# Pinning TensorE's order in an attention stage, halving and spreading the w4 tiles, moving transposes ahead of projections, and warming the array

## The chip, the cores and the metric

The kernel runs on one core of a Trainium2 chip. The metric is the device time of one execution in microseconds (us). A time quoted below is the median of several executions. Each kernel also has a trace of one execution; its span is 1.6 to 1.8 us shorter than the time of that execution, because the span goes from the first to the last instruction only. Executions are sorted into a fast and a slow state (more than 1.5% above the fastest of the same kernel); ratios use fast ones, while the medians quoted hold all executions. Engines are named as in the profile: PE is TensorE, DVE is VectorE, ACT is ScalarE, SPq is the queue on which SyncE issues DMAs.

## The reference, cut to what matters

The input x has 2048 rows of 512. Two branches work on its layer norm: a local dilated attention (32 heads of 16, each query sees 8 keys at distance 0, 2, ..., 14), and a gated MLP.

```python
x  = A_x
xn = _layernorm(x)
s  = _A_ref(xn, A_wqkv, A_wo)         # q,k,v = xn @ wqkv; softmax over 8 keys; @ wo
g  = _silu(_B_ref(xn, B_w1, B_w2, B_w3, B_w4))
return x + s * g
# _B_ref: h = gelu(layernorm(x) @ w1); h shifted by rows; x1 = x + h @ w2
#         return x1 + gelu(layernorm(x1) @ w3) @ w4      (w3: 512 x 1376, w4: 1376 x 512)
```

## The kernel before

Because the dilation is 2, even and odd rows never meet in the attention, so the kernel splits x into two halves of 1024 rows (`p` = 0, 1). It has three stages.

1. For four chunks of 512 rows: layer norm on DVE, transposes on PE, the q/k projection, w1, w2, a second layer norm, w3.
2. The attention: 9 units for each half, 18 in all. A unit has 128 or 120 queries, the last of a half only 56. PE computes v (4 matmuls) and scores (16 small matmuls in four groups of 4). ACT takes the exponential of each group, DVE multiplies by the mask, and PE computes AV, the weighted values (32 small matmuls), whose result is copied out by ACT (first half of the heads) and DVE (second half). The 16 tiles of w4 (12 matmuls each) are woven in so that PE has work while ACT computes.
3. The tail: 16 output tiles with wo, the gate and the residual on DVE, and the stores.

The softmax's denominators come out of AV as extra rows. A "run" of units is normalised together: the denominators are stored to DRAM, loaded in another layout (`dn`), inverted on DVE (`rb`), stored, and loaded back as a broadcast (`rr`); a later DVE multiply on `oT` (`normalise_end`) applies them. `load_xo` loads 1 MB of x again for the residual of the tail. The library's scheduler may reorder instructions of one engine unless told otherwise.

```python
for cuts in ((0, 5, NU), (0, 5, 7, NU)):          # runs: five in all
    ...
sm4 = tc.tile_pool(name="sm4", bufs=5)            # prob and others
psA = tc.tile_pool(name="psA", bufs=3, space=PSUM)   # s_ps, o_ps
psB = tc.tile_pool(name="psB", bufs=2, space=PSUM)   # v_ps, w4_ps, wo_ps
...
def weighted(p, u, va, prs):
    ...
    op = psa("o_ps")
    for jj in range(2):
        for dt in range(ND):
            for cg in range(4):
                nc.tensor.matmul(op[32*cg : 32*cg+32, jj, dt*nq : (dt+1)*nq], ...)   # 16 per jj
        dst = orw[p][jj][:, :, q0 - ra : q0 - ra + nq]
        if jj == 0:
            nc.scalar.activation(dst, src, AF.Copy)
        else:
            nc.vector.tensor_copy(out=dst, in_=src)
    if u == runs[p][r][1] - 1:
        normalise(p, r)

def normalise(p, r):
    for jj in range(2):
        nc.sync.dma_start(out=hv[jj], in_=orw[p][jj][DH : P : 32, :, 0:rw])
    nc.sync.dma_start(out=dn, in_=den_d...)
    ...
    nc.vector.reciprocal(out=rb, in_=dn)
    nc.sync.dma_start(out=rden_d..., in_=rb)
    for dt in range(ND):
        nc.sync.dma_start(out=rr[:, dt, 0:rw], in_=rden_d[8*dt : 8*dt+8, :]...broadcast)

def normalise_end(p, r):
    nc.vector.tensor_tensor(out=oT..., in0=oT..., in1=rrs[p, r]..., op=ALU.mult)
...
fill = {n: [w4s[n]] for n in range(13)}           # one whole w4 tile in each of units 0 to 12
fill[5].append(lambda: load_xo(0))
fill[9].append(lambda: load_xo(1))
fill[9].append(lambda: normalise_end(0, 0))
fill[13] = [lambda: normalise_end(0, 1)]
fill[17] = [lambda: normalise_end(1, 0)]
prev = None
for n, (p, u) in enumerate(order):
    cur = (p, u) + scores(p, u)                   # v, then the scores
    for f in fill.get(n, ()):
        f()
    if prev is not None:
        weighted(*prev)                           # AV of the unit before
    prev = cur
weighted(*prev)
for f in w4s[13:]:
    f()                                           # the last three w4 tiles
```

The softmax here doesn't subtract the row's maximum and nothing guards it: scores larger than these inputs give would overflow.

## Time and profile before

The kernel took 259.66 us, the median of three executions (258.02 to 260.58). The stages are read from PE's timeline: the first matmul of the attention and the first of wo bound the second stage.

| what | before |
|---|---|
| traced span | 258.0 us |
| stage 1, until the first attention matmul | 119.5 us |
| stage 2, attention and w4 | 115.6 us |
| stage 3, from the first wo matmul to the end | 22.9 us |

From the page of the kernel before: PE's busy time with its share of the span and number of instructions; the busy share of PE and the clock granted to it in 40 slices of 6.45 us, in tenths (9 is 90% or more); and the start of the line about the chain of work that ended last.

```profile
PE 222.5 (86%) x1704; PEld 98.3 (38%) x1704; DVE 152.8 (59%) x275; ACT 136.0 (53%) x164; POOL 39.9 (15%) x82
...
PE   0399898958999999999999999785999988799882
...
PEclk9999999997999999999999999998699999569999
...
PE 56%; DVE 15%; ACT 10%; DMA 9%; issue 4%; POOL 3%; SPq 2%; DVEq 0%; ACTq 0%
```

PE is the engine to look at: 86% busy, and most of the chain. But it is not at its best: the start is empty, some slices in the attention show 8, 7 or less, and the clock falls to 8, 6 and 5 in places (a matmul then takes longer and still counts as busy: ten w4 matmuls behind a fall are busy 4.45 us instead of 2.33, as shown below). So the busy share says little here about how far the kernel is from its best: the change below took 6% off the time and moved the busy share only from 86% to 88%.

From PE's timeline of the kernel before, in stage 1. Columns: start and length in us, engine, line, operation, output<-inputs, size, number of instructions grouped; in brackets the idle time before and what ended it.

```profile
13.66 8.84 PE L234 MATMUL qk_ps<-xnT_133,wqk_sb 128*128 128x512 bf16 x30
...
58.37 0.27 PE L222 MATMUL rrep_ps<-diag,ones_bf 128*128 128x128 bf16 x2 [3.12 <-DVE xnT_134 L215]
59.03 3.17 PE L234 MATMUL qk_ps<-xnT_134,wqk_sb 128*128 128x512 bf16 x7 [0.40 <-DVE xnT_134 L215]
```

PE's first work, 16 transposes, comes at 8.86 us, and the first projections run slowly (30 matmuls in 8.84 us, 0.29 each; later ones take 0.22). Their starts are 0.43 us apart until about 18 us and 0.21 us after. The clock row does not show this (it has 9 in these slices), so a cold start has to be read from durations. At 58 us PE has nothing to do for 3.12 us because the transposed data of the last chunk have not been copied out of PSUM by DVE.

The same view, over one unit of the attention with a whole w4 tile.

```profile
141.77 0.39 PE L397 MATMUL o_ps<-prob,v_aug_129 128*32 128x120 bf16 x16
142.09 0.82 PE L349 MATMUL v_ps<-wv_sb,xnT_133 128*128 128x512 bf16 x3
142.98 0.39 PE L397 MATMUL o_ps<-prob,v_aug_129 128*32 128x120 bf16 x16
...
144.52 0.39 PE L327 MATMUL w_ps<-w_sb,h3T 128*128 128x512 bf16 x1
145.07 0.38 PE L369 MATMUL s_ps<-qm_137,kT_135 32*128 32x240 bf16 x4 [0.17 <-ACT prob L376]
145.38 2.33 PE L327 MATMUL w_ps<-w_sb,h3T 128*128 128x512 bf16 x10
```

The AV matmuls (`o_ps`) come in two groups of 16 with v between them. The w4 tile sits mostly behind all the scores (x10). Between the score groups there is one w4 matmul. One such unit takes 6.1 us.

DVE's timeline of the kernel before, around PE's largest hole in the attention.

```profile
174.34 1.43 DVE L447 TENSOR_TENSOR oT_1500<-oT_1500,rr 128x2432 bf16<-128x2432 bf16 x1 [2.83 <-DMA rr<-rden_d_1502]
175.68 0.65 DVE L408 CAST orw<-o_ps 128x480 bf16<-128x480 f32 x1
176.25 0.67 DVE L353 CAST v_aug_129<-v_ps 64x512 bf16<-64x512 f32 x1
```

PE's timeline at the same place:

```profile
176.98 0.81 PE L349 MATMUL v_ps<-wv_sb,xnT_134 128*128 128x512 bf16 x3 [2.54 <-DVE v_aug_129 L353]
...
180.83 4.45 PE L327 MATMUL w_ps<-w_sb,h3T 128*128 128x512 bf16 x10
```

DVE works in order here: it waited 2.83 us for the broadcast load `rr` with the copies of AV and v behind it (at 175.68 and 176.25), so PE had a hole of 2.54 us. After the hole ten w4 matmuls took 4.45 us, against 2.33 us in an undisturbed unit: the granted clock over 180 to 190 us is 0.73.

### The profile page before, as it was taken

To read this page: it belongs to the slowest core of one execution; us is meant where nothing else is said; L and a number is where in the kernel's file an instruction comes from. 1 tells how busy PE (TensorE), PEld (TensorE's weight loads), DVE (VectorE), ACT (ScalarE), POOL (GpSimd) and SP (SyncE) were. 2 spreads that over 40 slices of the span, in tenths; PEclk is the share of its full clock that TensorE was granted. 3 is DMA by queue.
4 is the path that set the end of the run, shared out by engine and by line. 5 is a ranking of instruction groups with operands and counts; after the bars stand their busy time and mean duration, and the time that the engine had idled before them with its cause. 6 is when DMAs were issued, how large, how long until landed. Compare 5 with 4: busy or idle time off the path is not lost.

```text
span 258.0 us, 4290 instructions
## 1 busy us (share of the span) xinstructions
PE 222.5 (86%) x1704; PEld 98.3 (38%) x1704; DVE 152.8 (59%) x275; ACT 136.0 (53%) x164; POOL 39.9 (15%) x82
## 2 busy tenths in 40 slices
PE   0399898958999999999999999785999988799882
PEld 0334444433444444444334433232333333334330
DVE  6688815087069571001766776538566977936994
ACT  1037575702813436567977777464477899603000
POOL 1526320001001110000000006000050006514100
PEclk9999999997999999999999999998699999569999
DMA  6998000002301734102200006160042005232343
GB/s 193 363 400 295 3 0 0 3 0 81 81 0 40 206 81 125 40 1 69 94 3 0 3 1 105 45 229 0 3 76 73 0 3 104 59 96 59 100 150 122
DMA packets 27628, 21.31 MB, mean 83 GB/s; under 512 B 12184, under 2 KB 26712, under 8 KB 27608
## 3 DMA queue, kind: packets, MB, share of 16 engines
q1 hardware_dynamic: 24152, 16.85, 21.0%
q0 software_dynamic: 1280, 2.10, 4.7%
q10 hardware_dynamic: 2176, 2.10, 2.3%
q8 instruction: 13, 0.21, 0.4%
q14 instruction: 7, 0.06, 0.1%
HBM read 12.39 MB, written 4.46 MB: 65 GB/s over the span
## 4 chain that ended last, share of the span: by engine, by line
PE 56%; DVE 15%; ACT 10%; DMA 9%; issue 4%; POOL 3%; SPq 2%; DVEq 0%; ACTq 0%
PE w_ps L311 14%; PE w_ps L327 13%; PE qk_ps L234 9%; ACT prob L376 7%; PE w_ps L278 5%; PE w_ps L250 4%; PE s_ps L369 4%; DVE l1s L179 3%; DMA rr<-rden_d_1502 2%; PE o_ps L397 2%; PE v_ps L349 2%; DVE orw L408 2%; SPq L439 1%; DMA oT_2286<-orw 1%; ACT orw L406 1%
## 5 line engine op out<-in xcount | busy, mean ns | idle before, releaser
L376 ACT ACTIVATE prob<-s_ps 128x960 bf16<-128x960 f32 (+2 forms) x72 | 61.8, 951 | 18.2 <-PE s_ps L369 15.2
L327 PE MATMUL w_ps<-w_sb,h3T 128*128 128x512 bf16 (+1 forms) x176 | 49.1, 412 | 0.2
L379 DVE TENSOR_TENSOR prob<-prob,mask_126 128x1920 bf16<-128x1920 bf16 (+1 forms) x32 | 34.8, 1088 | 16.7 <-ACT prob L376 16.6
L311 PE MATMUL w_ps<-x1nT,w_sb 128*128 128x512 bf16 (+1 forms) x176 | 38.3, 379 | 0.0
L316 ACT ACTIVATE h3T<-w_ps 128x1024 bf16<-128x1024 f32 x20 | 20.5, 1023 | 25.6 <-PE w_ps L311 23.3
L311 PEld LDWEIGHTS <-w_sb 128*128 128x128 bf16 (+1 forms) x176 | 17.6, 100 | 20.4
L327 PEld LDWEIGHTS <-h3T 128*128 128x128 bf16 (+1 forms) x176 | 16.1, 102 | 22.6 <-issue 9.4
L429 POOL DMA_DIRECT2D oT_1500<-orw x16 | 8.3, 526 | 86.3 <-ACT orw L406 86.3
L234 PEld LDWEIGHTS <-wqk_sb 128*128 128x128 bf16 x128 | 13.4, 107 | 18.3 <-issue 5.0
L353 DVE CAST v_aug_129<-v_ps 128x512 bf16<-128x512 f32 (+1 forms) x9 | 6.1, 681 | 23.0 <-PE v_ps L349 23.0
L333 ACT ACTIVATE sig<-w_ps 128x512 bf16<-128x512 f32 x16 | 9.6, 600 | 17.5 <-PE w_ps L331 17.4
L234 PE MATMUL qk_ps<-xnT_133,wqk_sb 128*128 128x512 bf16 x64 | 17.0, 428 | 1.1 <-DVE xnT_133 L215 1.1
L429 POOL DMA_DIRECT2D oT_2286<-orw x24 | 12.1, 512 | 36.9 <-ACT orw L406 35.2
L240 ACT ACTIVATE qm_137<-qk_ps,hmask 128x1024 bf16<-128x1024 f32 x8 | 8.4, 1112 | 17.7 <-PE qk_ps L234 17.7
L234 PE MATMUL qk_ps<-xnT_134,wqk_sb 128*128 128x512 bf16 x64 | 16.1, 409 | 0.7 <-DVE xnT_134 L215 0.7
L283 DVE TENSOR_TENSOR xn_85<-w_ps,xn_85 128x1024 bf16<-128x1024 f32 x4 | 4.9, 1216 | 18.4 <-PE w_ps L278 18.4
L369 PE MATMUL s_ps<-qm_138,kT_136 32*128 32x240 bf16 (+2 forms) x144 | 12.6, 278 | 3.5 <-ACT prob L376 1.7
L240 ACT ACTIVATE qm_138<-qk_ps,hmask 128x1024 bf16<-128x1024 f32 x8 | 8.3, 1114 | 13.6 <-PE qk_ps L234 13.6
L250 PE MATMUL w_ps<-xn2T,w_sb 128*128 128x512 bf16 x64 | 14.5, 379 | 0.0
L408 DVE CAST orw<-o_ps 128x480 bf16<-128x480 f32 (+2 forms) x18 | 11.2, 625 | 3.6 <-PE o_ps L397 3.0
L349 PE MATMUL v_ps<-wv_sb,xnT_134 128*128 128x512 bf16 (+1 forms) x36 | 11.1, 385 | 2.5 <-DVE v_aug_129 L353 2.5
L369 PE MATMUL s_ps<-qm_137,kT_135 32*128 32x240 bf16 (+2 forms) x144 | 10.2, 260 | 3.0 <-DVE orw L408 1.6
(107 smaller groups left out, 284.3 us busy)
## 6 DMA issues: line engine op xcount, KB each, us to landing
w_sb<-in_B_w_dram SPq DMA_DIRECT2D x1, 1376.0 KB
w_sb<-in_B_w_dram SPq DMA_DIRECT2D x1, 1280.0 KB
xn_85<-in_A_x_dram SPq DMA_DIRECT2D x4, 256.0 KB, 7.1
wqk_sb<-in_A_wqkv_dram SPq DMA_DIRECT2D x2, 512.0 KB
w_sb<-in_B_w_dram SPq DMA_DIRECT2D x2, 512.0 KB
xn_86<-in_A_x_dram SPq DMA_DIRECT2D x4, 256.0 KB
xo_1463<-in_A_x_dram SPq DMA_DIRECT2D x1, 1024.0 KB
xo_1830<-in_A_x_dram SPq DMA_DIRECT2D x1, 1024.0 KB
```

Of the source, the lines that this page charges most:

```text
L234: nc.tensor.matmul(pt[:, b, :], lhsT=wqk_sb[:, dt, nt * P : (nt + 1) * P], rhs=xnT[p][:, dt, cs], start=(dt == 0), stop=(dt == ND - 1),)
L240: nc.scalar.activation(qm[p][:, 2 * a : 2 * a + 2, e, cs], pt, AF.Copy, scale=hmask[:, e : e + 1])
L250: nc.tensor.matmul(pt[:, b, :], lhsT=w1_sb[:, dt, g * P : (g + 1) * P], rhs=xn2T[:, dt, :], start=(dt == 0), stop=(dt == ND - 1),)
L311: nc.tensor.matmul(pt[:fs, ft % 2, :], lhsT=w3_sb[:, dt, ft * P : ft * P + fs], rhs=x1nT[:, dt, :], start=(dt == 0), stop=(dt == ND - 1),)
L316: last["gelu"] = nc.scalar.activation(h3T[:, 2 * a : 2 * a + 2, :], pt, AF.Gelu_apprx_tanh)
L327: nc.tensor.matmul(pt, lhsT=h3T[:fs, ft, jj * P : (jj + 1) * P], rhs=w4_sb[:fs, ft, :], start=(ft == 0), stop=False,)
L349: nc.tensor.matmul(vp[:nk, :], lhsT=xnT[p][:, dt, k0 : k0 + nk], rhs=wv_sb[:, dt, :], start=(dt == 0), stop=(dt == ND - 1),)
L369: nc.tensor.matmul(st[:nk, b, dl * 2 * nq : (dl + 1) * 2 * nq].rearrange("k (e q) -> k e q", e=2), lhsT=kT[p][r : r + 32, dt, k0 : k0 + nk ...
L376: nc.scalar.activation(prv[:nk, jj], st[:nk, :, 0 : 4 * nq], AF.Exp, scale=SCALE)
L379: nc.vector.tensor_tensor(out=ph[:nk], in0=ph[:nk], in1=msk[:nk, 0:nq].unsqueeze(1).to_broadcast([nk, 16, nq]), op=ALU.mult,)
L408: nc.vector.tensor_copy(out=dst, in_=src)
L429: nc.gpsimd.dma_start(out=oT[p][DH * hh : DH * (hh + 1), :, ra : ra + rw], in_=orw[p][jj][32 * cg : 32 * cg + DH, :, 0:rw],)
```

## The change

It has four intents: warm the array before the data arrive; put the transposes of the next chunk ahead of the projections of the current one, so that DVE's copies are hidden; split each w4 tile in two and spread the halves over all units; and fix PE's order in the attention (`pin` queues an instruction behind the one traced before it on its engine) with AV as one group of 32. It also normalises in six runs rather than five, and asks for the multiplies earlier after their runs. The diff, cut to its core:

```diff
-    for cuts in ((0, 5, NU), (0, 5, 7, NU)):
+    for cuts in ((0, 4, 7, NU), (0, 4, 7, NU)):
-    sm4 = ... bufs=5
+    sm4 = ... bufs=6
@@ loads of the first chunk: four of 128 KB instead of two of 256 KB
+        n = 1 if c == 0 else 2
+        for t0 in range(k * TPC, (k + 1) * TPC, n):
@@ warm-up
+    wm = psA.tile([P, 2, CH], F32, name="warm_ps", tag="a")
+    for i in range(16):
+        nc.tensor.matmul(wm[:, i % 2, :], lhsT=ones_bf[:], rhs=ones_bf...broadcast to 512, ...)
@@ stage_a is split: stage_a1 = transposes, rrep, xn2T; stage_a2 = q/k projection, w1
     stage_ln(0)
-    stage_a(0)
+    stage_a1(0)
     stage_ln(1)
+    stage_a1(1)
+    stage_a2(0)
     stage_ln(2)
-    stage_a(1)
+    stage_a1(2)
+    stage_a2(1)
     ...
@@ attention
+    def pin(ins):
+        return tc.keep_in_program_order(ins)
     # all v, score, AV, w4 and wo matmuls: nc.tensor.matmul(...) -> pin(nc.tensor.matmul(...))
     # w4_tile returns [half(0, NF // 2), half(NF // 2, NF)]: 5 matmuls, then 6 + 1
     # scores(p, u) -> values(p, u) and scores(p, u, dd) for two groups each
@@ weighted: both AV halves, then both copies
+        for jj in range(2):
             dst = orw[p][jj][:, :, q0 - ra : q0 - ra + nq]
...
+    halves = [h for w in w4s for h in w]
+    NH = 28
+    fill = {n: ([], []) for n in range(2 * NU)}
+    for i in range(NH):
+        m = i * 36 // NH
+        fill[m // 2][m % 2].append(halves[i])
+    fill[6][1].append(lambda: load_xo(0))
+    fill[10][1].append(lambda: load_xo(1))
+    fill[7][1].append(lambda: normalise_end(0, 0))
+    fill[10][1].append(lambda: normalise_end(0, 1))
+    fill[12][1].append(lambda: normalise_end(0, 2))
+    fill[16][1].append(lambda: normalise_end(1, 0))
+    va = values(*order[0])
     for n, (p, u) in enumerate(order):
-        cur = (p, u) + scores(p, u)
-        for f in fill.get(n, ()):
-            f()
+        prs = [scores(p, u, 0)]
+        for f in fill[n][0]:
+            f()
+        prs.append(scores(p, u, 1))
+        for f in fill[n][1]:
+            f()
         if prev is not None:
             weighted(*prev)
-        prev = cur
+        prev = (p, u, va, prs)
+        if n + 1 < len(order):
+            va = values(*order[n + 1])
```

More of the change, by code (lines that the diff above doesn't have):

```diff
@@ L73 @@
     sm5 = ctx.enter_context(tc.tile_pool(name="sm5", bufs=4))
-    sm4 = ctx.enter_context(tc.tile_pool(name="sm4", bufs=5))
+    sm4 = ctx.enter_context(tc.tile_pool(name="sm4", bufs=6))
     fin = ctx.enter_context(tc.tile_pool(name="fin", bufs=2))
@@ L95 @@
         p, k = c // 2, c % 2
-        for h in range(2):
-            t0 = k * TPC + 2 * h
+        n = 1 if c == 0 else 2
+        for t0 in range(k * TPC, (k + 1) * TPC, n):
             nc.sync.dma_start(
-                out=xn[p][:, t0 : t0 + 2, :],
-                in_=xv[p, t0 * P : (t0 + 2) * P, :].rearrange("(i q) d -> q i d", q=P),
+                out=xn[p][:, t0 : t0 + n, :],
+                in_=xv[p, t0 * P : (t0 + n) * P, :].rearrange("(i q) d -> q i d", q=P),
             )
@@ L130 @@
     nc.vector.memset(nhalf[:], -0.5)
+    wm = psA.tile([P, 2, CH], F32, name="warm_ps", tag="a")
+    for i in range(16):
+        nc.tensor.matmul(
+            wm[:, i % 2, :], lhsT=ones_bf[:], rhs=ones_bf.unsqueeze(1).to_broadcast([P, TPC, P]),
+            start=True, stop=True,
+        )
     hmask = const.tile([P, 2], F32, name="hmask")
@@ L200, in stage_ln, with stage_a1 @@
         r2s[c] = r2
-    def stage_a(c):
+    xn2Ts = {}
+    def stage_a1(c):
         p, k = c // 2, c % 2
@@ L228, in stage_a, with stage_a2 @@
         )
+        xn2Ts[c] = xn2T
+    def stage_a2(c):
+        p, k = c // 2, c % 2
+        cs = slice(k * CH, (k + 1) * CH)
+        xn2T = xn2Ts.pop(c)
         for a in range(ND):
@@ L318, in stage_w3, with half @@
                 last["gelu"] = nc.scalar.activation(h3T[:FL, NF - 1, :], pt[:FL, 0, :], AF.Gelu_apprx_tanh)
+    def pin(ins):
+        return tc.keep_in_program_order(ins)
     def w4_tile(c, jj):
         p, i = c // 2, (c % 2) * TPC + jj
-        h3T = h3[c]
-        pt = psB.tile([P, D], F32, name="w4_ps", tag="b")
-        for ft in range(NF):
-            fs = P if ft < NF - 1 else FL
-            nc.tensor.matmul(
-                pt, lhsT=h3T[:fs, ft, jj * P : (jj + 1) * P], rhs=w4_sb[:fs, ft, :],
-                start=(ft == 0), stop=False,
-            )
-        nc.tensor.matmul(pt, lhsT=ident[:], rhs=xn[p][:, i, :], start=False, stop=True)
-        sig = fin.tile([P, D], BF16, name="sig", tag="sig")
-        nc.scalar.activation(sig, pt, AF.Tanh, scale=0.5)
-        nc.vector.scalar_tensor_tensor(
-            out=xn[p][:, i, :], in0=sig, scalar=1.0, in1=pt, op0=ALU.add, op1=ALU.mult
-        )
+        st = {}
+        def half(lo, hi):
+            if lo == 0:
+                st["pt"] = psB.tile([P, D], F32, name="w4_ps", tag="b")
+            pt = st["pt"]
+            for ft in range(lo, hi):
+                fs = P if ft < NF - 1 else FL
+                pin(
+                    nc.tensor.matmul(
+                        pt, lhsT=h3[c][:fs, ft, jj * P : (jj + 1) * P], rhs=w4_sb[:fs, ft, :],
+                        start=(ft == 0), stop=False,
+                    )
+                )
+            if hi == NF:
+                pin(nc.tensor.matmul(pt, lhsT=ident[:], rhs=xn[p][:, i, :], start=False, stop=True))
+                sig = fin.tile([P, D], BF16, name="sig", tag="sig")
+                nc.scalar.activation(sig, pt, AF.Tanh, scale=0.5)
+                nc.vector.scalar_tensor_tensor(
+                    out=xn[p][:, i, :], in0=sig, scalar=1.0, in1=pt, op0=ALU.add, op1=ALU.mult
+                )
+        return [lambda: half(0, NF // 2), lambda: half(NF // 2, NF)]
     cnt = {"v": 0}
@@ L341, with values @@
     orw = {}
-    def scores(p, u):
+    def values(p, u):
         q0, nq, k0, nk = units[u]
@@ L348, in scores @@
         for dt in range(ND):
-            nc.tensor.matmul(
-                vp[:nk, :], lhsT=xnT[p][:, dt, k0 : k0 + nk], rhs=wv_sb[:, dt, :],
-                start=(dt == 0), stop=(dt == ND - 1),
+            pin(
+                nc.tensor.matmul(
+                    vp[:nk, :], lhsT=xnT[p][:, dt, k0 : k0 + nk], rhs=wv_sb[:, dt, :],
+                    start=(dt == 0), stop=(dt == ND - 1),
+                )
             )
@@ L355, in scores @@
         )
+        return va
+    def scores(p, u, dd):
+        q0, nq, k0, nk = units[u]
         msk = mask0 if u == 0 else mask1
-        prs = []
-        for t in range(4):
-            dd, jj = t // 2, t % 2
-            if jj == 0:
-                pr = sm4.tile([P, H * P // 2], BF16, name="prob", tag="s4")
-                prv = pr[:, 0 : H * nq // 2].rearrange("p (t b x) -> p t b x", t=2, b=2)
-                prs.append(pr)
+        pr = sm4.tile([P, H * P // 2], BF16, name="prob", tag="s4")
+        prv = pr[:, 0 : H * nq // 2].rearrange("p (t b x) -> p t b x", t=2, b=2)
+        for jj in range(2):
             st = psa("s_ps")
@@ L368, in scores @@
                     dt = 2 * dd + dl
-                    nc.tensor.matmul(
-                        st[:nk, b, dl * 2 * nq : (dl + 1) * 2 * nq].rearrange("k (e q) -> k e q", e=2),
-                        lhsT=kT[p][r : r + 32, dt, k0 : k0 + nk],
-                        rhs=qm[p][r : r + 32, dt, :, q0 : q0 + nq],
-                        start=True, stop=True, tile_position=(r, 0),
+                    pin(
+                        nc.tensor.matmul(
+                            st[:nk, b, dl * 2 * nq : (dl + 1) * 2 * nq].rearrange("k (e q) -> k e q", e=2),
+                            lhsT=kT[p][r : r + 32, dt, k0 : k0 + nk],
+                            rhs=qm[p][r : r + 32, dt, :, q0 : q0 + nq],
+                            start=True, stop=True, tile_position=(r, 0),
+                        )
                     )
@@ L376, in scores @@
                 nc.scalar.activation(prv[:nk, jj], st[:nk, :, 0 : 4 * nq], AF.Exp, scale=SCALE)
-            if jj == 1:
-                ph = pr[:, 0 : 16 * nq].rearrange("p (h q) -> p h q", q=nq)
-                nc.vector.tensor_tensor(
-                    out=ph[:nk], in0=ph[:nk],
-                    in1=msk[:nk, 0:nq].unsqueeze(1).to_broadcast([nk, 16, nq]), op=ALU.mult,
-                )
-        return va, prs
+        ph = pr[:, 0 : 16 * nq].rearrange("p (h q) -> p h q", q=nq)
+        nc.vector.tensor_tensor(
+            out=ph[:nk], in0=ph[:nk],
+            in1=msk[:nk, 0:nq].unsqueeze(1).to_broadcast([nk, 16, nq]), op=ALU.mult,
+        )
+        return pr
     def weighted(p, u, va, prs):
@@ L396, in weighted @@
                     pi = jj * 8 + b * 4 + (dt % 2) * 2 + e
-                    nc.tensor.matmul(
-                        op[32 * cg : 32 * cg + 32, jj, dt * nq : (dt + 1) * nq],
-                        lhsT=va[:nk, dt * 8 + 4 * jj + cg, :],
-                        rhs=prs[dt // 2][:nk, pi * nq : (pi + 1) * nq],
-                        start=True, stop=True, tile_position=(0, 32 * cg),
+                    pin(
+                        nc.tensor.matmul(
+                            op[32 * cg : 32 * cg + 32, jj, dt * nq : (dt + 1) * nq],
+                            lhsT=va[:nk, dt * 8 + 4 * jj + cg, :],
+                            rhs=prs[dt // 2][:nk, pi * nq : (pi + 1) * nq],
+                            start=True, stop=True, tile_position=(0, 32 * cg),
+                        )
                     )
+        for jj in range(2):
             dst = orw[p][jj][:, :, q0 - ra : q0 - ra + nq]
@@ L459, in final_tile @@
         for dt in range(ND):
-            nc.tensor.matmul(
-                pt, lhsT=oT[p][:, dt, i * P : (i + 1) * P], rhs=wo_sb[:, dt, :],
-                start=(dt == 0), stop=(dt == ND - 1),
+            pin(
+                nc.tensor.matmul(
+                    pt, lhsT=oT[p][:, dt, i * P : (i + 1) * P], rhs=wo_sb[:, dt, :],
+                    start=(dt == 0), stop=(dt == ND - 1),
+                )
             )
@@ L474 @@
     stage_ln(0)
-    stage_a(0)
+    stage_a1(0)
     stage_ln(1)
+    stage_a1(1)
+    stage_a2(0)
     stage_ln(2)
-    stage_a(1)
+    stage_a1(2)
+    stage_a2(1)
     stage_ln(3)
-    stage_a(2)
+    stage_a1(3)
+    stage_a2(2)
     stage_b(0)
-    stage_a(3)
+    stage_a2(3)
     stage_b(1)
@@ L489 @@
     stage_w3(3)
-    w4s = [lambda c=c, jj=jj: w4_tile(c, jj) for c in range(NCH) for jj in range(TPC)]
-    fill = {n: [w4s[n]] for n in range(13)}
-    fill[5].append(lambda: load_xo(0))
-    fill[9].append(lambda: load_xo(1))
-    fill[9].append(lambda: normalise_end(0, 0))
-    fill[13] = [lambda: normalise_end(0, 1)]
-    fill[17] = [lambda: normalise_end(1, 0)]
+    w4s = [w4_tile(c, jj) for c in range(NCH) for jj in range(TPC)]
+    halves = [h for w in w4s for h in w]
[10 more added lines that the diff above has]
+    fill[16][1].append(lambda: normalise_end(1, 0))
     order = [(p, u) for p in range(2) for u in range(NU)]
+    va = values(*order[0])
     prev = None
     for n, (p, u) in enumerate(order):
-        cur = (p, u) + scores(p, u)
-        for f in fill.get(n, ()):
+        prs = [scores(p, u, 0)]
[3 more added lines that the diff above has]
+        for f in fill[n][1]:
             f()
@@ L506 @@
             weighted(*prev)
-        prev = cur
+        prev = (p, u, va, prs)
+        if n + 1 < len(order):
+            va = values(*order[n + 1])
+    for h in halves[NH : NH + 2]:
+        h()
     weighted(*prev)
-    for f in w4s[13:]:
-        f()
+    for h in halves[NH + 2 :]:
+        h()
     for i in range(M // P):
```

## The prediction

> **What bounds the kernel now.** TensorE: 222.5 of 258.0 us busy on the page, the chain of waits 56% PE. Three stages, from the PE timeline:
> 1. 0 to 119.5 us, projections, MLP up to w3. The first transposes wait until 8.9 us. The array then starts cold: 16 transposes take 1.89 us (1.06 later), 30 qk matmuls 8.84 us (6.64 later). Before each next chunk's projections PE waits for transpose copies on DVE (0.34+0.33 us twice; 3.12+0.40 us at 54 to 59 us).
> 2. 119.5 to 235.1 us, attention with w4. A unit with a whole w4 tile takes 6.1 us: about 5.4 us PE, the rest waits for exp (0.16), the DVE copy of the AV result (0.2 to 0.5), and the second AV half behind ScalarE's copy of the first (0.24). Units 13 to 16 have no w4 and go at 3.9 us, bound by ScalarE (4 exp at 0.86 plus a copy). After low PE use or the 2.5 us hole at 174.5 us the granted clock falls (0.73 in 180-190, 0.51 in 220-230): ten w4 matmuls take 4.45 us instead of 2.33. The hole is DVE waiting in order for the normalisation's broadcast load (to 174.3).
> 3. The tail, 22.9 us: 16 output tiles, bound by DVE (0.60+0.35 us each), and the last store.
>
> **What the change does.**
> Stage 1: 16 dummy matmuls before the data arrive (ones ready at 1.06 us) take no time that is needed and warm the array: -3 us. [...] Transposes ahead of projections hide the copies: -5 us. Smaller first loads: -0.5 us. DVE must normalise chunks 1 and 2 earlier and is nearly full there, so I give back 1 us. Together about -8 us.
> Stage 2: 28 w4 halves over 36 slots instead of 13 tiles in units 0 to 12 and three at the end. By durations above, a unit costs PE about 4.4 us on average (v 0.97, scores 2x0.32, AV 0.65, w4 9.3x0.216, switches), ScalarE 4.3, DVE 4.4. No engine has slack, so I expect about 4.9 us per full unit, 81 us for all, plus 3 us start and 6 us of w4 and AV after: 90 us. Against it: normalisation now is six runs; its DVE operations stand in order about one unit after the DMAs start, while the chain store-load-reciprocal-store-broadcast took 12.5 us here. I expect DVE to stand 2 to 4 us several times, worst at the second run of half 0, whose multiply follows the third run's copies. PE sees about half, and one or two stalls may still drop the clock for about 10 us (4 us lost each). So 101 us instead of 115.6: -14 us.
> Stage 3: unchanged, within 1 us.
>
> Only PE gaps, cold matmuls and throttling go away; the work is equal.
>
> **Predicted: 238 us, 80% between 230 and 248. Faster by over 2%: 0.95; within 2%: 0.04; slower: 0.01.**
>
> **Checks.** First qk matmuls at 0.22 us each, first attention matmul near 111 us; PE busy through 10 to 111 us without gaps. Full attention units 4.6 to 5.5 us; granted clock above 0.9 in most attention slices; longest DVE waits at the reciprocal and the normalisation multiply. Tail 21 to 24 us.
>
> **What would make it wrong.** Normalisation waits of DVE exposed in full (up to 15 us), with throttling after each: 248 us or more. Waits hidden and clock kept: 230 us. If pinning makes PE stand behind a late AV group, units stay at 6 us.

The terms of stage 1 come to -3 - 5 - 0.5 + 1 = -7.5, rounded to -8. The -3 us of the warm-up agree with the durations listed under 1 (1.89 - 1.06 and 8.84 - 6.64, together 3.03 us). The 10 us at a low clock behind a stall, with 4 us lost, are the author's estimate; the trace of the kernel before shows means of 0.73 and 0.51 over 10 us each, which makes 2.7 and 4.9 us of full clock lost.

## More of the kernel before

SyncE's DMA queue of the kernel before (the length is the issuing time only):

```profile
165.60 0.39 SPq L455 DMA_DIRECT2D xo_1830<-in_A_x_dram  x1
166.04 2.54 SPq L439 DMA_DIRECT2D rr<-rden_d_1502  x4
```

## The result, and the profile after

The changed kernel took 244.34 us (median of four, 242.17 to 245.36); the kernel before took 259.51 us in the same rounds. The ratio is 0.9408, with a 95% interval of 0.9329 to 0.9487: faster. A ratio here is the mean time of one kernel's fast runs over that of the other's fast runs of the same rounds, so it is not quite the ratio of the medians that are quoted. The outputs agree with the reference.

| stage | before | after | difference | predicted difference |
|---|---|---|---|---|
| 1 | 119.5 | 109.8 | -9.7 | -8 |
| 2 | 115.6 | 110.6 | -5.0 | -14 |
| 3 | 22.9 | 22.2 | -0.7 | 0 |
| span | 258.0 | 242.6 | -15.4 | -22 |

So the total fell into the predicted range, but the second stage gave a third of what was expected of it. From the page after, the lines that answer to those above (slices of 6.07 us).

```profile
PE 213.3 (88%) x1720; PEld 93.2 (38%) x1720; DVE 152.0 (63%) x277; ACT 136.1 (56%) x164; POOL 43.0 (18%) x90
...
PE   8789999999999999999788983998797897699892
...
PEclk9999999999999999999999998699979999889999
...
PE 48%; DMA 18%; DVE 13%; ACT 7%; issue 5%; SPq 5%; POOL 2%; DVEq 0%; ACTq 0%
```

PE's slices 4 to 19 are now full, but the second half still has 7s and 8s, a 3 in slice 25 (146 to 152 us), and the clock still drops to 6 once. In the chain PE's share fell from 56% to 48%, and that of DMA rose from 9% to 18%: the chain now goes through transfers. That is the first hint of where the expected gain went.

PE's timeline after, in stage 1.

```profile
1.12 6.14 PE L134 MATMUL warm_ps<-ones_bf 128*128 128x512 bf16 x16 [1.12 <-DVE ones_bf L128]
8.16 1.36 PE L222 MATMUL tr_ps<-ident,xn_85 128*128 128x128 bf16 x16 [0.90 <-DVE xn_85 L203]
...
11.89 5.12 PE L249 MATMUL qk_ps<-xnT_152,wqk_sb 128*128 128x512 bf16 x23
18.12 0.40 PE L222 MATMUL tr_ps<-ident,xn_85 128*128 128x128 bf16 x4 [1.10 <-DVE xn_85 L203]
```

The dummies fill 1.12 to 7.26 us, and the first projections run at 5.12/23 = 0.22 us each. The last chunk's projections (32 matmuls from 51.09 to 58.00 us) follow without a gap; the hole of 3.12 us is gone. PE's busy time by windows shows the sum. From its first transpose to the attention PE was busy 104.3 of 110.6 us before, and 99.3 of 101.6 us after. So of the 9.7 us, 0.7 are the earlier first transpose (8.86 to 8.16), 4.1 less waiting, and 4.9 shorter work at a better clock.

A unit of the attention after, in the same view.

```profile
130.17 0.60 PE L428 MATMUL o_ps<-prob,v_aug_148 128*32 128x120 bf16 x32
130.82 1.02 PE L377 MATMUL v_ps<-wv_sb,xnT_152 128*128 128x512 bf16 x4
131.77 0.39 PE L399 MATMUL s_ps<-qm_156,kT_154 32*128 32x240 bf16 x8
133.00 0.59 PE L399 MATMUL s_ps<-qm_156,kT_154 32*128 32x240 bf16 x8 [0.84 <-DVE orw L441]
```

AV is one group of 32, v follows whole, and the w4 half (x6, from 133.52 us, 1.47 us long) sits where the change put it. Nothing moves into the 0.84 us in which the second pair of score groups waits for a PSUM buffer that DVE's copy of AV has to free. Keep that wait in mind for one of the experiments.

DVE's timeline after, around its longest DMA wait of the attention.

```profile
147.81 0.92 DVE L468 RECIPROCAL rb<-dn 128x122 bf16<-128x122 bf16 x1 [4.41 <-DMA dn<-den_d_1417]
148.64 2.16 DVE L409 TENSOR_TENSOR prob<-prob,mask_145 128x1920 bf16<-128x1920 bf16 x2
150.72 1.22 DVE L441 CAST orw<-o_ps 128x480 bf16<-128x480 f32 x2
...
156.10 1.18 DVE L480 TENSOR_TENSOR oT_1416<-oT_1416,rr 128x1952 bf16<-128x1952 bf16 x1 [1.90 <-DMA rr<-rden_d_1418]
```

PE's timeline at the same place:

```profile
146.98 0.38 PE L399 MATMUL s_ps<-qm_156,kT_154 32*128 32x240 bf16 x4
151.42 0.58 PE L399 MATMUL s_ps<-qm_156,kT_154 32*128 32x240 bf16 x4 [4.07 <-DVE orw L441]
151.94 2.74 PE L350 MATMUL w_ps<-w_sb,h3T 128*128 128x512 bf16 x6
```

DVE stood 4.41 us at the reciprocal. Its next operations, two masks and two AV copies, ran back to back as soon as it went on; at 156.10 it waited 1.90 us more, for `rr`. PE's next score group waited 4.07 us for one of those copies. Then the six w4 matmuls took 2.74 us, against 1.47 in the unit shown before, at a clock of 0.68 (150 to 160 us). Why was `dn` late? The timeline of SyncE's DMA queue after (here the length is the issuing time only):

```profile
138.70 0.44 SPq L488 DMA_DIRECT2D xo_1566<-in_A_x_dram  x1
141.49 0.34 SPq L458 DMA_DIRECT2D dn<-den_d_1417  x1
```

The chain of work over this stretch, in order of time (start and length in us, what; a DMA's length runs to its landing):

```profile
138.13 3.30 DMA den_d_1417<-orw
...
141.49 6.30 DMA dn<-den_d_1417
```

The 1 MB residual load was issued at 138.70, and the small `dn` load at 141.49 took 6.30 us until DVE could start. In the kernel before, `dn` loads took 1.8 to 2.4 us to landing. The other multiplies of the attention waited too, each for its `rr`: 1.90, 2.17, 2.47 and 2.19 us. In sum DVE waited about 14 us for DMAs in the attention, against 7.5 us before.

### The profile page after: what moved, and what is told of

It reads as the page before. It is cut to its first block, busy times and chain, and to the rows that moved or that the text cites. A ratio compares the mean times of both kernels' runs of the same rounds, so it can differ in the third digit from the quotient of the medians.

```text
span 242.6 us, 4350 instructions
## 1 busy us (share of the span) xinstructions
PE 213.3 (88%) x1720; PEld 93.2 (38%) x1720; DVE 152.0 (63%) x277; ACT 136.1 (56%) x164; POOL 43.0 (18%) x90
## 4 chain that ended last, share of the span: by engine, by line
PE 48%; DMA 18%; DVE 13%; ACT 7%; issue 5%; SPq 5%; POOL 2%; DVEq 0%; ACTq 0%
PE w_ps L326 15%; PE qk_ps L249 9%; ACT prob L407 6%; PE w_ps L293 6%; PE w_ps L265 6%; PE w_ps L350 5%; SPq L472 3%; DVE prob L409 3%; DMA xn_85<-in_A_x_dram 3%; DMA dn<-den_d_1417 3%; PE v_ps L377 2%; DMA dn<-den_d_1877 2%; PE wo_ps L494 2%; PE s_ps L399 1%; DMA rr<-rden_d_1418 1%
## 5 line engine op out<-in xcount | busy, mean ns | idle before, releaser
L407 ACT ACTIVATE prob<-s_ps 128x960 bf16<-128x960 f32 (+2 forms) x72 | 62.5, 930 | 20.0 <-PE s_ps L399 19.9
L350 PE MATMUL w_ps<-w_sb,h3T 128*128 128x512 bf16 (+1 forms) x176 | 46.5, 403 | 3.2 <-DVE xn_85 L359 2.4
L409 DVE TENSOR_TENSOR prob<-prob,mask_145 128x1920 bf16<-128x1920 bf16 (+1 forms) x32 | 34.5, 1085 | 10.8 <-ACT prob L407 10.6
L462 POOL DMA_DIRECT2D oT_1416<-orw x24 | 12.3, 522 | 73.4 <-ACT orw L439 73.2
L350 PEld LDWEIGHTS <-h3T 128*128 128x128 bf16 (+1 forms) x176 | 15.8, 101 | 24.3 <-issue 11.4
L462 POOL DMA_DIRECT2D oT_2229<-orw x24 | 12.1, 512 | 38.9 <-ACT orw L439 38.0
L249 PEld LDWEIGHTS <-wqk_sb 128*128 128x128 bf16 x128 | 12.1, 98 | 12.8
L249 PE MATMUL qk_ps<-xnT_152,wqk_sb 128*128 128x512 bf16 x64 | 15.4, 379 | 0.8 <-DVE xnT_152 L224 0.8
L249 PE MATMUL qk_ps<-xnT_153,wqk_sb 128*128 128x512 bf16 x64 | 14.5, 379 | 0.0
L399 PE MATMUL s_ps<-qm_156,kT_154 32*128 32x240 bf16 (+2 forms) x144 | 8.8, 271 | 6.2 <-DVE orw L441 5.7
L377 PE MATMUL v_ps<-wv_sb,xnT_153 128*128 128x512 bf16 (+1 forms) x36 | 9.9, 399 | 3.6 <-DVE xn_86 L359 3.6
L399 PE MATMUL s_ps<-qm_157,kT_155 32*128 32x240 bf16 (+2 forms) x144 | 9.2, 265 | 3.6 <-ACT prob L407 2.4
```

What stands on the lines that cost most here:

```text
L249: nc.tensor.matmul(pt[:, b, :], lhsT=wqk_sb[:, dt, nt * P : (nt + 1) * P], rhs=xnT[p][:, dt, cs], start=(dt == 0), stop=(dt == ND - 1),)
L350: nc.tensor.matmul(pt, lhsT=h3[c][:fs, ft, jj * P : (jj + 1) * P], rhs=w4_sb[:fs, ft, :], start=(ft == 0), stop=False,)
L377: nc.tensor.matmul(vp[:nk, :], lhsT=xnT[p][:, dt, k0 : k0 + nk], rhs=wv_sb[:, dt, :], start=(dt == 0), stop=(dt == ND - 1),)
L399: nc.tensor.matmul(st[:nk, b, dl * 2 * nq : (dl + 1) * 2 * nq].rearrange("k (e q) -> k e q", e=2), lhsT=kT[p][r : r + 32, dt, k0 : k0 + nk ...
L407: nc.scalar.activation(prv[:nk, jj], st[:nk, :, 0 : 4 * nq], AF.Exp, scale=SCALE)
L409: nc.vector.tensor_tensor(out=ph[:nk], in0=ph[:nk], in1=msk[:nk, 0:nq].unsqueeze(1).to_broadcast([nk, 16, nq]), op=ALU.mult,)
```

## The experiments

The leading theory was that the missing 9 us are normalisation waits: DVE works in order (at 147.81 us above, masks and copies ran behind the 4.41 us wait), the change asks for reciprocals and multiplies before their data have landed, and the 1 MB load makes one of them much later. The rival was that the pinned order itself costs: PE stands behind a late AV or score group and nothing may move forward. Smaller questions were what the warm-up, stage 1 and the spreading of the halves are worth. Three calls ran on three different chips; the kernel before ran with each (medians 259.24, 259.20 and 258.76 us), so medians of different calls are comparable to about half a microsecond. Stage times come from one traced execution of each kernel, which varies too: the two traces of the changed kernel have 110.6 and 109.1 us in stage 2, and in the 12 traces that have the new stage 1 with the warm-up the attention starts at 109.6 to 110.9 us.

### e1_no_warm: the change without the dummies

```diff
-    wm = psA.tile([P, 2, CH], F32, name="warm_ps", tag="a")
-    for i in range(16):
-        nc.tensor.matmul(wm[:, i % 2, :], ...)
```

> The changed kernel without the 16 dummy matmuls. Theory (the dummies only warm the array while the data arrive): the 16 first transposes take about 1.9 us again and the first thirty qk matmuls about 8.8 us, attention starts 2 to 3.5 us later than the 109.8 us of the changed kernel, 247 us in all. Rival (the dummies buy nothing; stage 1 gains by its order alone, or DVE bounds the start): attention starts within 1 us of 109.8 us, 244 us.

Measured: 245.0 us, ratio 0.9454 (0.941 to 0.9499); the attention starts at 111.67 us instead of 109.8. PE's timeline of this run:

```profile
13.14 7.07 PE L242 MATMUL qk_ps<-xnT,wqk_sb 128*128 128x512 bf16 x23
```

The same 23 projections take 7.07 us instead of 5.12, and the 16 transposes 1.89 instead of 1.36. But the warm kernel then waits 1.10 us at 18.12 (shown above) and 0.41 us at 20.54, because DVE has not finished the next chunk; the cold one does not wait there. The warm-up brings 1.9 us at the start of the attention against the changed kernel's trace, and 0.8 to 2.1 against all twelve; that is just short of the 2 to 3.5 us of the theory and more than its rival allowed. In the total time the intervals of the two kernels overlap, so it is not resolved there. The 1.9 us are 0.8% of the span of 243 us.

### e2_stage1_only: the new stage 1 with the old attention

```diff
 (on the kernel before)
+ four first loads, the 16 dummies, stage_a1/stage_a2 in the new order
```

> The new stage 1 (dummies, smaller first loads, transposes ahead of projections) with the attention stage of the kernel before (its order, its runs, five buffers in the shared pool). Theory (the two parts add up; stage 1 is worth 9.7 us and attention 5): attention starts near 110 us and takes 115 us as before, 249 to 250 us in all. Rival (the parts need each other, the old attention starting earlier runs into later loads or another throttle phase): below 246 or above 253 us.

Measured: 248.23 us, ratio 0.9576 (0.9531 to 0.9622); two of its six executions were slow, and the four fast ones lie between 247.84 and 248.33 us. The trace is of a slow execution (251.73 us), so only its start is used: the attention begins at 109.82 us. So stage 1 is worth 11 us of the time, 1 us more than the stage table says and than was expected, and the new attention only about 4 to 5 us. Within that the parts add up; the missing gain is in the attention.

### e3_xo_late: the residual loads behind the last normalisation of half 0

```diff
-        nc.sync.dma_start(out=xo[p], ...)
+        pin(nc.sync.dma_start(out=xo[p], ...))
-    fill[6][1].append(lambda: load_xo(0))
-    fill[10][1].append(lambda: load_xo(1))
+    fill[12][1].append(lambda: load_xo(0))     # behind normalise_end(0, 2)
+    fill[12][1].append(lambda: load_xo(1))
```

> The changed kernel with both residual loads (1 MB each) pinned behind the broadcast of the third run of half 0, that is after about 182 us instead of at 138.7 and 170.1 us. Theory (the 4.4 us wait of DVE for the first denominator load is that load queueing behind the 1 MB transfer, and the half clock after it follows from the hole): that wait falls below 1 us, the 4.1 us hole of TensorE at 147 to 151 us is gone, and so is the low clock after it; 6 us less, 238 us. Rival (the denominator load is slow by itself, or behind the AV copies of the other queue): it still takes over 4 us from issue to landing, 243 to 244 us.

Measured: 241.45 us, ratio 0.9283 (0.9223 to 0.9343), stage 2 108.1 us. This gained 2 to 3 us, not 6: a miss. The `dn` waits shrank to 0.7 us in all, so the load was the cause of the long one. But DVE now reached the next operation of the chain earlier, and waited there. DVE's timeline:

```profile
152.26 1.18 DVE L480 TENSOR_TENSOR oT<-oT,rr 128x1952 bf16<-128x1952 bf16 x1 [3.28 <-DMA rr<-rden_d]
```

PE has a hole of 3.24 us, up to 155.16, behind it. The wait was handed on from the reciprocal to the multiply.

### e5_xo_norm_late: the loads late, and each multiply one unit later

```diff
 (on e3_xo_late; the multiply in normalise_end is pinned on DVE as well)
-    fill[7][1].append(lambda: normalise_end(0, 0))
-    fill[10][1].append(lambda: normalise_end(0, 1))
-    fill[12][1].append(lambda: normalise_end(0, 2))
-    fill[16][1].append(lambda: normalise_end(1, 0))
+    fill[8][1].append(lambda: normalise_end(0, 0))
+    fill[11][1].append(lambda: normalise_end(0, 1))
+    fill[13][1].append(lambda: normalise_end(0, 2))
+    fill[17][1].append(lambda: normalise_end(1, 0))
```

> As the one before, and the normalisation multiplies of the first four runs pinned one unit later in the order of DVE. Theory (the 1.9 to 2.5 us waits of DVE for the broadcast loads cost TensorE 1 to 3 us each): these waits vanish, units 9 to 17 lose their excess, 4 to 7 us less than with the late loads alone, 232 us. Rival (the waits are slack that DVE would spend waiting for exp anyway): within 1.5 us of the late loads alone.

Measured: 235.65 us, ratio 0.9081 (0.9037 to 0.9126), stage 2 99.4 us, mean granted clock of the profiled run 0.993 (0.970 after). DVE's timeline at the same two operations as above:

```profile
145.15 0.92 DVE L468 RECIPROCAL rb<-dn 128x122 bf16<-128x122 bf16 x1 [0.67 <-DMA dn<-den_d]
...
158.11 1.16 DVE L481 TENSOR_TENSOR oT<-oT,rr 128x1952 bf16<-128x1952 bf16 x1
```

The reciprocal waits 0.67 us (its `dn` was issued at 142.25, so 2.90 us from issue to use instead of 6.30), and the multiply does not wait at all. All DMA waits of DVE in the attention sum to 1.9 us. The gain over e3 is 5.8 us, in the expected 4 to 7. The theory holds, and a comparison of the time from one unit's v to the next one's v shows where. Between the changed kernel and this one, 13 of the 17 intervals are equal to 0.02 us, and four are not:

| interval from this unit's v to the next one's | after | e5 | where DVE waited in the changed kernel |
|---|---|---|---|
| 7 | 11.92 | 6.06 | reciprocal and multiply of run 0 of half 0, then slowed w4 matmuls |
| 11 | 6.29 | 5.69 | multiply of run 1 |
| 12 | 7.06 | 6.12 | multiply of run 2 |
| 16 | 8.28 | 6.06 | multiply of run 0 of half 1 |
| sum of all 17 | 99.85 | 90.23 | |

That is 9.6 us in four places, 5.9 of them at one. The rest of the 11.2 us is behind the last unit's v (10.8 and 9.2 us). The small ones must not be read too closely: in the second trace of the changed kernel (a_after_again) the same four are 11.36, 5.30, 7.14 and 8.23 us. Interval 11 is there shorter than in e5: DVE waited only 0.86 us for that multiply, against 2.17, and the clock stayed at 1.00 over 170 to 180 us, where it was 0.85. The large ones, 7 and 16, are the same in both traces to 0.6 us.

### e4_norm_late: the multiplies late, the loads early as in the change

```diff
 (on e5_xo_norm_late)
+    fill[6][1].append(lambda: load_xo(0))
+    fill[10][1].append(lambda: load_xo(1))
-    fill[12][1].append(lambda: load_xo(0))
-    fill[12][1].append(lambda: load_xo(1))
```

(The pin on the loads was taken off again too.)

> The later normalisation multiplies alone; the 1 MB residual loads stay early as in the changed kernel. Against the run with both edits (235.65 us) it tells what the early loads cost once no other wait follows. Theory (the first load delays the denominator load, TensorE stands some 4 us, and the clock falls after the hole): 5 to 7 us more, 241 to 242 us, with the 4 us wait at the first reciprocal and the low clock after it back. Rival (the late loads gave only the 3 us that they gave alone, because DVE has slack): 238.5 us or less.

Measured: 241.33 us, ratio 0.9327 (0.9278 to 0.9377), stage 2 104.4 us. With 5.7 us more than e5, the early 1 MB load costs what the theory says even when no multiply is in the way. The reciprocal waited 4.30 us again, PE's hole is 3.97 us long, up to 151.07, and the reciprocal behind the second 1 MB load waited 2.28 us.

### e6b_no_pin: e5 with PE's order left to the scheduler

```diff
 (on e5_xo_norm_late; DMA and DVE pins stay)
     def pin(ins):
+        if ins.ins.engine == nc.tensor.engine:
+            return ins
         return tc.keep_in_program_order(ins)
```

> As the run with late loads and late multiplies, but TensorE's instructions are not pinned; the scheduler orders them and moves single matmuls between score groups. Theory (pinning is only the means; what counts is that the AV copies stand behind both AV halves and that the w4 halves are spread, and both stay): within 1.5 us of 235.65 us. Rival (pinning itself is worth something, the free order puts scores that wait for exp ahead of matmuls that could run): 239 us or more.

Measured: 231.72 us, ratio 0.8963 (0.8922 to 0.9004), stage 2 95.4 us. It was expected to be equal, and by its rival slower; it is 4 us faster, which neither foresaw, and which speaks for the rival named at the head of this section: the pinned order costs. PE's timeline of e5 in one unit:

```profile
170.47 0.38 PE L399 MATMUL s_ps<-qm,kT 32*128 32x240 bf16 x4 [1.05 <-ACT prob L407]
171.34 0.38 PE L399 MATMUL s_ps<-qm,kT 32*128 32x240 bf16 x4 [0.48 <-ACT prob L407]
171.65 1.25 PE L350 MATMUL w_ps<-w_sb,h3T 128*128 128x512 bf16 x5
```

PE's timeline of this run in the same unit:

```profile
167.09 0.81 PE L352 MATMUL w_ps<-w_sb,h3T 128*128 128x512 bf16 x3 [0.29 <-DVE xn L361]
167.85 0.38 PE L401 MATMUL s_ps<-qm,kT 32*128 32x240 bf16 x4
168.16 0.60 PE L352 MATMUL w_ps<-w_sb,h3T 128*128 128x512 bf16 x2
168.71 0.38 PE L401 MATMUL s_ps<-qm,kT 32*128 32x240 bf16 x4
```

In the pinned order each of the last two score groups stands for ACT's exponential, 1.05 and 0.48 us, and the five w4 matmuls come behind them; the scheduler runs the same five before and between the groups, where they fill these waits. The two units from there take 11.8 us in e5 and 10.4 in e6b (the clock dip in e5 that is named under e9 falls into these two and is part of it). Elsewhere the scheduler runs v ahead of AV, which had waited 0.58 us for ACT. Not every move pays: the third unit is 0.19 us longer than in e5. PE's waits in the attention fell: of the scores for ACT's exponential from 2.4 to 1.0 us, of the scores for the AV copy from 4.0 to 2.2, of w4 for a buffer from 3.2 to 2.1. All its waits there, wo's left out, sum to 11.5 us in e5 and to 7.2 here, which is the gain of 4 us.

### a_after_again and e6_no_pin: the changed kernel, and it without PE pins

```diff
 (e6_no_pin, on the changed kernel)
     def pin(ins):
-        return tc.keep_in_program_order(ins)
+        return ins
```

> The changed kernel once more, unaltered, as a control on the chip of the three others and with more rounds: 243 to 245.5 us, ratio 0.935 to 0.945. Outside of that, the other ratios of earlier calls must not be compared to within 1%.

> The changed kernel with nothing altered but the pins of TensorE taken off (early residual loads and early multiplies stay). Theory (pinning costs some 4 us, as it did with the waits taken out: a pinned half tile may not move one matmul ahead to cover a wait of the scores): 2 to 5 us less than the control. Rival (with the normalisation waits in place, units stand on DVE anyway, and pins cost nothing or shield from a worse order): within 1.5 us of the control or slower.

Measured: the changed kernel 243.06 us (0.9398, 0.9352 to 0.9445), as expected of the control; without pins 244.83 us (0.9452, 0.9414 to 0.949), where the theory expected 2 to 5 us less, so its rival was right. Here the pins cost nothing that can be resolved. So the price of the pins can be seen only once the normalisation waits are gone. The long waits hid the short ones here (taking the pins off changed the time by +1.8 us in e6_no_pin and by -3.9 in e6b), and an experiment on the changed kernel alone would have cleared the pins.

### e7u_split_av: ACT's copy of AV between its halves again

```diff
 (on e6b_no_pin, in weighted)
-        for jj in range(2):
             dst = orw[p][jj][:, :, q0 - ra : q0 - ra + nq]     # again inside the loop of the matmuls
```

> The run without pins, with late loads and late multiplies (231.7 us), but ScalarE's copy of the first AV half again stands between the two halves, so that the second half waits for it, as in the kernel before. Theory (each unit loses the wait that the kernel before showed, 0.24 us after filling, or up to 0.5): 4 to 9 us more, 236 to 241 us, AV groups of 16 again with values matmuls between them. Rival (values matmuls fill the wait): below 233.5 us.

Measured: 235.73 us, ratio 0.9104 (0.907 to 0.9138), stage 2 99.0 us: 4 us slower than e6b, just under what was expected. With the copy between, the scheduler again makes AV groups of 16, with v or scores between them, in most units. But the reason is not the expected wait of the second half: PE's waits in the attention sum to 4.4 us, less than e6b's 7.2, and PE is busy longer, 93.3 us against 88.7 in e10, which has e6b's order and no records missing. So the whole AV group is a part of the change that pays, and it needs the copies' place in the program, not the pins.

### e8_whole_tiles and e9_front: where the w4 work sits

```diff
 (e8_whole_tiles, on e5_xo_norm_late: both halves of a tile behind all scores, in 14 of 18 units)
-        m = i * 36 // NH
-        fill[m // 2][m % 2].append(halves[i])
+        fill[(i // 2) * 18 // 14][1].append(halves[i])
```

```diff
 (e9_front, on e5_xo_norm_late: two halves in each of units 0 to 12, none in 13 to 17)
-    NH = 28
+    NH = 26
-        m = i * 36 // NH
-        fill[m // 2][m % 2].append(halves[i])
+        fill[i // 2][i % 2].append(halves[i])
```

(In e9_front all halves that are left follow the last AV.)

> As the run with late loads and late multiplies, but whole w4 tiles in 14 of the 18 units, behind all four score groups, instead of halves between them. Theory (a half tile between the score groups covers the wait of the second pair for exp to free a PSUM buffer): each unit with a tile shows a wait of the scores of 0.5 to 1 us for exp or the AV copy, 14 units make 5 to 10 us, 241 to 246 us. Rival (the waits are only moved; ScalarE gets its scores sooner and the next unit gains what this one loses): within 2 us of 235.65 us.

> As the run with late loads and late multiplies, but two halves in each of units 0 to 12 and none in 13 to 17, three tiles at the end, as the kernel before had its tiles. Theory (units with two halves take 5.6 us, bound by TensorE, units without one about 4.0, bound by ScalarE; sum 13x5.6 + 5x4.0 + one more tile 2.6 against 99.5 us now, and TensorE's low use in units 13 to 17 brings the low clock back): 3 to 7 us more, 239 to 243 us. Rival (spreading does not matter, as each engine's total is the same): within 1.5 us.

Measured: e8 247.45 us (0.9554, 0.9501 to 0.9608), 11.8 us over e5 and a little above the expected 241 to 246; stage 2 111.0 us. PE's waits of that run in the attention (us in total, times, longest):

```profile
PE s_ps L399 <- ACT prob L407: 13.8, 18, 1.7
```

In e5 the same wait sums to 2.4 us. With the tile behind all scores PE runs the four groups in one go and stands for ACT. The half between the groups is what feeds both engines.

e9 measured 242.14 us (0.9375, 0.9329 to 0.9421), 6.5 us over e5; stage 2 105.9 us. The total is as expected. Of the four units without w4 two take 4.0 and 4.2 us, at ACT's pace, though PE has less to do; then the clock falls and the next two take 5.9 and 6.0 us. From the view by windows, the stretch of 190 to 196 us (length, then busy us of PE, PE's weight loads, DVE, ACT and POOL, each with its number of instructions, then the granted clock, the DMA share and GB/s):

```profile
190.00:196.00 6.00, 4.05 (x52) 1.81 (x52) 4.50 (x5) 3.56 (x4) 0.57 (x2) 0.50 0.28 49
```

At a clock of 0.50 an AV group takes 0.99 us instead of 0.60. The clock fell at 189.35 us, and no idle time of PE from 182 us to there is longer than 0.95 us, so here the clock fell with short gaps alone ahead of it. e5, with halves in these units, kept 1.00 over the same stretch (it had one dip of its own, 0.83 over 170 to 180 us). What the traces do show is the load. The low spells of the clock (0.50) in stages 1 and 2 are 3.41, 6.83 and 10.24 us long before and 6.83, 3.41 and 3.41 us after, so the load is taken here over 3.41 us. In the 3.41 us ahead of the fall in e9 PE was busy 53% (some of e9's matmul records are missing, so it may be a little more). In the kernel before, the 3.41 us ahead of the three falls in stages 1 and 2 were busy 9, 45 and 75%, in the kernel after 34, 55 and 41%; with these stages cut into stretches of that length, none of the others at full clock was busy less than 59% before and 57% after (those of the cold start left out). So five of these six falls and the one in e9 followed 3.41 us with PE busy 55% or less; the one at 75% (219.48 us, in the units without w4) stays unexplained. That the load is the cause is not shown.

### e10_act_tail: the best version with part of the tail moved to ACT

```diff
 (on e6b_no_pin)
-        nc.vector.tensor_tensor(out=sg, in0=pt, in1=xn[p][:, i, :], op=ALU.mult)
+        nc.scalar.activation(sg, pt, AF.Copy)
+        nc.vector.tensor_tensor(out=sg, in0=sg, in1=xn[p][:, i, :], op=ALU.mult)
-            nc.scalar.dma_start(
+            (nc.scalar if (p, i) == (1, M // P - 1) else nc.gpsimd).dma_start(
```

> The run without pins, with late loads and late multiplies (231.7 us), and in the tail ScalarE, idle there, copies each output tile from PSUM to bf16 in SBUF, so that DVE multiplies from SBUF (output stores go by the other queue except the last). Theory (the tail is bound by DVE at 0.60+0.35 us a tile; from SBUF the multiply takes about 0.35 us): the tail falls from 24 us to 20 to 22, 228 to 230.5 us. Rival (the tail is bound by the normalisation chain of the last run, whose multiply waited 1.9 us): within 1 us of 231.7 us.

Measured: 231.07 us, ratio 0.8924 (0.8891 to 0.8957), against 0.8963 of e6b: within the intervals, so the rival was right and the tail did not become shorter by the expected 2 to 4 us (23.5 us, 24.3 in e6b). DVE's multiply became shorter (0.42 instead of 0.68 us busy), but the tail is then held by the last run's multiply, for which PE waits 2.27 us. Its chain starts late, as SyncE's DMA queue shows:

```profile
206.87 2.53 SPq L474 DMA_DIRECT2D rr<-rden_d  x4
209.44 1.12 SPq L457 DMA_DIRECT2D den_d<-orw  x2
```

The denominators' store of the last run is issued directly behind the four issues of the `rr` load of the run before, which occupy the queue for 2.53 us. The last run's multiply starts only at 222.08 us; whether its `rr` or DVE's other work, which ends at 221.94, held it to the last is not shown. This or e6b is the fastest version found: about 231 us, 11% under the kernel before and 5% under the change.

## Why the prediction was right or wrong

- **Total.** Predicted 238 us in a range of 230 to 248; measured 244.3. The direction and the range held; the middle was 6 us too low.
- **Stage 1, predicted -8, measured -9.7.** Right in kind. The warm-up was taken as 3 us and is worth about 1.9 (e1), because DVE's layer norm of the next chunk then becomes the limit for 1.5 us. Matmuls became fast 5.1 us after the first dummy, and in the kernel before about 5.5 us after the first projection. The transposes were taken as 5 us less 1 given back, and gave about 7 (what is left of 9.7 less 1.9 and 0.7; not run alone). What was missed is that the clock was low behind the old hole at 58 us (0.50 over 59.05 to 62.47 us): the 32 projections there spread over 8.71 us (59.03 to 67.74) against 6.91 us after (51.09 to 58.00), another 1.8 us.
- **Stage 2, predicted 101 us (90 plus 11 of stalls), measured 110.6.** This is the step that failed. The stalls were sized well as a sum, 11 us: taking them away (e5) gave 9.7 to 11.2 us, by the two traces of the changed kernel. That sum is partly luck, since more than half of it lay at one place that the prediction did not name. The mis-sized term is the base of 90, "about 4.9 us per full unit, 81 us for all, plus 3 us start and 6 us". With the waits gone, e5 still needs 99.4: the 16 intervals of full units sum to 86.6 us (5.4 each), the small one between the halves takes 3.6, and from the last unit's v to wo it is 9.2. A rate of 4.9 with 81 us for 18 units left 1.3 us for each small unit. Of the 9.4 us too much, 4 are the pinned order (e6b: 95.4 us). The prediction took the change's order as the one that reaches the average load of the engines and did not cost what a fixed order loses where a score group has to wait. The other 5 us are the average load itself, put too low: it was taken as 4.4 us of PE per unit, and in e10, which has e6b's order and all matmul records, PE is busy 4.75 us per full unit, 5.6 us more over 16 of them; ACT is busy 4.5 us, where 4.3 was taken.
- **Which stall is worst.** Predicted: the multiply of the second run of half 0. Measured: the reciprocal of the first run, 4.41 us, with 1.90 us more at its multiply. The prediction did not look at what the move of the residual load does: it was put on the queue ahead of `dn`. e3 and e4 show that it costs 4 us of DVE wait; with both its causes removed (e5), the loss is gone.
- **Clock.** "One or two stalls may still drop the clock": it dropped to 0.68 (150 to 160 us), to 0.85 (170 to 180) and once more, for 3.41 us, at 211.05. In the kernel after the clock fell at 149.61, 2.3 us into the hole of 4.07 us, and the old kernel's hole of 2.54 us was already followed by a clock of 0.73. In the 3.41 us ahead of the falls PE was busy 34, 55 and 41% after and 9, 45 and 75% before (under e9).
- **DVE's order.** In the trace DVE kept its order: two masks whose exponentials ACT had ended at 146.28 ran only at 148.64, after the 4.41 us.
- **Tail.** Predicted within 1 us; measured 0.7 us shorter.
- **Open.** Six runs instead of five, the sixth `sm4` buffer and the smaller first loads were not tried alone. How much of e6b's gain is w4 matmuls moved ahead of waiting score groups and how much is other reordering was not separated.

## What to carry to other kernels

When an engine that works in order must consume a DMA's result, place the consumer by the measured latency of the whole chain, and look at what else was put on the queue just before: here one 1 MB load ahead of a small one and multiplies one unit too early cost about 9 of 244 us. Spread filler work so that it sits between the producer's groups (behind them it cost 11.8 us, e8), but leave the last steps of the order to the scheduler unless a trace shows that it errs (4 us, e6b); and test such a pin again after the long waits are gone, since they hide its price. Judge a change by stage: here the total hit the range while one stage's gain was overestimated nearly threefold.
